# Clustered attention followed by a gated FFN on one core: contiguous loads, a half-batch pipeline, mask rows without DMA, weights staged in fp32

## The chip, the core and the metric

The kernel runs on one NeuronCore of a Trainium2 chip. The metric is device time in microseconds (us), the median of several runs. Before the change it is 446.86 us (three runs, 446.13 to 447.54).

Engine names: PE multiplies matrices (PEld is its weight load), DVE is the vector engine, ACT the scalar engine, POOL the GpSimd engine. SP only issues DMAs; "SPq" and "POOLq" are the instruction queues from which DMAs are issued.

## The reference

```python
B, H, S, D = 4, 8, 768, 64          # 16 clusters per head
q_assign = argmax(q_n @ c_n.T)      # cluster of each query (normalised vectors)
k_assign = argmax(k_n @ c_n.T)
scores   = where(q_assign[:, None] == k_assign[None, :], q @ k.T / 8, -1e9)
attn     = softmax(scores)
x        = (attn @ v) as (3072, 512)
out      = (silu(x @ w_gate) * (x @ w_val)) @ w_out     # d_ff 1536
```

All inputs are fp32. The three weight matrices are 9.4 MB together, q, k and v 18.9 MB.

## The kernel before

Work on PE comes in these pieces. A *head* is prepared by six transposes (q and k to feature-major). A *quad* of four heads is then routed: a matmul with the centroids, then a chain on DVE (transpose, maximum, compare, transpose back) that gives one-hot rows. These 16 rows are put under the 64 feature rows of q and of k, so that a single matmul of 80 rows gives the masked scores. A *unit* of attention is two score matmuls, one exp on ACT and two value matmuls. A head has three units for each half of the queries. A *half batch* is 24 units (8 heads), and it gives the 384 tokens of one FFN *chunk*. A chunk has 12 gate/value blocks (`gv`, 8 matmuls each) and 3 output blocks (`o_ps`, 12 matmuls each).

```python
def load_quad(qi):                       # q and k share one tile, interleaved
    for i in range(4):
        t = sb.tile([128, J, 2, 64], FP32, tag="qk", bufs=6)
        nc.sync.dma_start(out=t[:, :, 0, :], in_=q[b, h].rearrange("(p j) d -> p j d", p=128))
        nc.sync.dma_start(out=t[:, :, 1, :], in_=k[b, h].rearrange("(p j) d -> p j d", p=128))
# ... v and the weights: nc.gpsimd.dma_start(bf16 tile <- fp32 dram), converted on the way
load_quad(0); load_v(0); load_quad(1)
# ... centroids; load_v(1); all weights
def prep_route(qi):
    # ... matmul with centroids, DVE: transpose, max, compare
    nc.vector.transpose(out=ohT, in_=oh)
    for i in range(4):                   # mask rows go to their partitions by DMA
        nc.sync.dma_start(out=qaug[(b, h)][D:KA], in_=ohT[32 * i:32 * i + NCL, :])
        nc.sync.dma_start(out=kaug[(b, h)][D:KA], in_=ohT[32 * i + NCL:32 * i + 2 * NCL, :])
# ... att_scores, att_values; per pair of heads:
                nc.vector.reciprocal(out=den, in_=den)          # 128 x 384
                nc.gpsimd.tensor_tensor(out=xall[...], in0=num, in1=den, op=ALU.mult)
# ... main program
for f in prep_work(0): f[0](*f[1:])      # both quads of batch 0
for b in range(B):
    ffn = list(ffn_work(b - 1)) if b > 0 else []     # FFN one whole batch behind
    for ui, u in enumerate(units):                   # 48 units
        pt = att_scores(u)
        want = len(ffn) * (ui + 1) // n              # paced by number of blocks
        # ... emit FFN blocks up to want; att_values of the unit before
        want = len(prep) * max(0, ui + 1 - 12) // (n - 12)   # preparation spread evenly
        # ...
for f in ffn_work(B - 1): f[0](*f[1:])   # two chunks alone at the end
```

The softmax here doesn't subtract the row's maximum and nothing guards it: scores larger than these inputs give would overflow.

## Time and profile before

| Stretch (span 444.2 us) | What runs | What limits it |
|---|---|---|
| 0 to 50.8 us | loads, preparation of the first two quads | loads |
| 50.8 to about 105 us | attention of batch 0, no FFN | ACT, 49.8 of 54.2 us busy |
| 105 to 397 us | attention beside the FFN of the batch before | PE, with bubbles |
| 397 to 444 us | FFN of the last batch | PE |

The page of the kernel before, second part: forty equal slices of 11.1 us. Each digit is the busy share in tenths; PEclk is the clock granted to PE. The line of packets stands below the slices.

```profile
...
PE   3601778889889998999889998998889988989996
...
ACT  3200499898678577765677777756776677633231
...
PEclk9955599999999999999999999999999999999999
DMA  9999893579001434652003122110000100010101
GB/s 158 193 208 198 164 148 73 84 87 133 18 1 36 125 63 64 91 82 58 19 1 73 71 19 29 8 48 29 14 0 26 47 1 1 25 47 2 71 1 71
DMA packets 83838, 28.77 MB, mean 65 GB/s; under 512 B 77152, under 2 KB 79712, under 8 KB 83808
...
```

PE does little in the first four slices while the DMA line is full, and the granted clock is half in the third to the fifth. Of 83,838 packets, 77,152 carry less than 512 B.

The table of windows of the kernel before: start and end, length, then busy us and number of instructions (PE, PEld, DVE, ACT, POOL), granted clock, DMA share, GB/s.

```profile
...
0.00:50.80 50.80, 16.38 (x78) 10.54 (x78) 9.34 (x13) 9.65 (x12) 30.74 (x52) 0.72 1.17 192
50.80:105.00 54.20, 46.66 (x273) 24.79 (x271) 34.59 (x34) 49.84 (x71) 28.45 (x34) 0.98 0.70 108
...
```

The timeline of the kernel before, from its first 64 us: start, duration, engine, line, operation, and in brackets the idle time before it with what ended it.

```profile
...
16.23 9.06 SPq L94 DMA_DIRECT2D qk<-in_k_dram  x1
...
20.16 0.98 DVE L192 STREAM_TRANSPOSE ohT<-oh 128x768 bf16<-128x768 bf16 x1
...
26.51 11.98 SPq L94 DMA_DIRECT2D qk<-in_k_dram  x1
...
29.82 0.84 POOL L158 CAST qa<-qkT 64x768 bf16<-64x768 f32 x1
...
38.59 3.96 SPq L196 DMA_DIRECT2D qa<-ohT  x1
...
47.95 1.51 PE L150 MATMUL tp<-ident_f,qk 128*128 128x128 f32 x6 [2.60 <-DMA qk<-in_k_dram]
...
50.83 0.82 PE L212 MATMUL sc<-qa,ka 80*128 80x384 bf16 x2
...
```

The one-hot rows of the first quad are ready at 21.1 us. The first copy that carries them leaves at 38.6 us, because two q, k loads ahead of it occupy the SP queue for 9.1 and 12.0 us. The first scores come at 50.8 us.

The reciprocal in the list of groups, and four lines of the chain that ended last, kernel before. A group line gives line, engine, operation, out<-in with shapes, count, busy us, mean ns.

```profile
...
L254 DVE RECIPROCAL den<-den 128x384 f32<-128x384 f32 x32 | 81.6, 2550 | 0.5
...
```

```profile
...
143.35 2.65 PE o_ps L294 x12
...
240.31 2.65 PE o_ps L294 x12
...
340.58 2.59 PE o_ps L294 x12
...
385.17 2.59 PE o_ps L294 x12
...
```

In the chain lines (start, duration, what), the same output block of one batch and the next lies 97.0 us apart (143.35 to 240.31), and in the last batch, which prepares nothing, the last two half batches lie 44.6 us apart (340.58 to 385.17).

**The ledger.** PE's least work is worked out from dense stretches of the timeline: 0.65 us a unit, 1.30 us a gate/value block, 2.6 us an output block, 0.85 us a head's transposes, 1.47 us a quad's routing. 192 units, 96 and 24 blocks, 32 heads and 8 quads make 351 us. A stretch's length less the least work done in it is PE time lost. A batch with preparation needs 88 us, a half batch without it 39 us. So the kernel before loses 4.5 us in each half batch with preparation and 5.6 us without.

### The profile page before, as it was taken

To read this page: it belongs to the slowest core of one execution; us is meant where nothing else is said; L and a number is where in the kernel's file an instruction comes from. 1 tells how busy PE (TensorE), PEld (TensorE's weight loads), DVE (VectorE), ACT (ScalarE), POOL (GpSimd) and SP (SyncE) were. 2 spreads that over 40 slices of the span, in tenths; PEclk is the share of its full clock that TensorE was granted. 3 is DMA by queue.
4 is the path that set the end of the run, shared out by engine and by line. 5 is a ranking of instruction groups with operands and counts; after the bars stand their busy time and mean duration, and the time that the engine had idled before them with its cause. 6 is when DMAs were issued, how large, how long until landed. Compare 5 with 4: busy or idle time off the path is not lost.

```text
span 444.2 us, 6000 instructions
## 1 busy us (share of the span) xinstructions
PE 374.1 (84%) x2152; PEld 206.8 (47%) x2152; DVE 257.3 (58%) x343; ACT 274.6 (62%) x412; POOL 123.2 (28%) x157
## 2 busy tenths in 40 slices
PE   3601778889889998999889998998889988989996
PEld 2301345454445555544455555544454545445552
DVE  4400166676877188655875287728675567558280
ACT  3200499898678577765677777756776677633231
POOL 9455504575002333531103133320000000000000
PEclk9955599999999999999999999999999999999999
DMA  9999893579001434652003122110000100010101
GB/s 158 193 208 198 164 148 73 84 87 133 18 1 36 125 63 64 91 82 58 19 1 73 71 19 29 8 48 29 14 0 26 47 1 1 25 47 2 71 1 71
DMA packets 83838, 28.77 MB, mean 65 GB/s; under 512 B 77152, under 2 KB 79712, under 8 KB 83808
## 3 DMA queue, kind: packets, MB, share of 16 engines
q1 hardware_dynamic: 55968, 20.52, 19.0%
q0 software_dynamic: 27840, 7.87, 16.8%
q8 instruction: 17, 0.28, 0.3%
q14 instruction: 13, 0.11, 0.1%
HBM read 28.38 MB, written 6.29 MB: 78 GB/s over the span
## 4 chain that ended last, share of the span: by engine, by line
PE 53%; ACT 17%; DVE 14%; SPq 6%; DMA 5%; issue 3%; POOL 1%; ACTq 0%; DVEq 0%; POOLq 0%
PE o_ps L294 12%; PE gv L269 12%; PE gv L274 11%; PE sc L212 7%; DVE den L254 7%; PE acc L234 6%; DMA qk<-in_k_dram 5%; ACT den L247 5%; SPq L94 3%; PE sp L169 3%; ACT pt_83 L218 3%; ACT pt_85 L218 3%; ACT pt_84 L218 2%; ACT th L279 2%; SPq L92 2%
## 5 line engine op out<-in xcount | busy, mean ns | idle before, releaser
L212 PE MATMUL sc<-qa,ka 80*128 80x384 bf16 x384 | 93.4, 326 | 7.1 <-ACT qkT L155 2.8
L269 PE MATMUL gv<-xall,wg_sb 128*128 128x384 bf16 x384 | 78.0, 325 | 17.9 <-ACT pt_83 L218 5.7
L279 ACT ACTIVATE th<-gv 128x384 f32<-128x384 f32 x96 | 47.1, 491 | 58.5 <-PE gv L274 55.2
L254 DVE RECIPROCAL den<-den 128x384 f32<-128x384 f32 x32 | 81.6, 2550 | 0.5
L282 DVE SCALAR_TENSOR_TENSOR ug<-th,gv 128x384 f32<-128x384 f32 x96 | 52.0, 547 | 50.5 <-ACT th L279 49.3
L255 POOL TENSOR_TENSOR xall<-num,den 128x384 bf16<-128x384 f32 x32 | 31.9, 997 | 175.1 <-DVE den L254 174.5
L274 PE MATMUL gv<-xall,wv_sb 128*128 128x384 bf16 x384 | 78.1, 326 | 0.0
L250 DVE TENSOR_SCALAR num<-acc 64x384 f32<-64x384 f32 x64 | 39.9, 623 | 60.8 <-ACT den L247 59.8
L294 PE MATMUL o_ps<-wo_sb,hT 128*128 128x512 bf16 x288 | 66.2, 379 | 1.0 <-DVE hT L285 0.9
L150 PE MATMUL tp<-ident_f,qk 128*128 128x128 f32 x192 | 31.9, 306 | 34.4 <-DMA qk<-in_k_dram 34.4
L269 PEld LDWEIGHTS <-wg_sb 128*128 128x128 bf16 x384 | 37.0, 96 | 49.9 <-issue 27.1
L212 PEld LDWEIGHTS <-ka 80*128 80x128 bf16 x384 | 36.9, 98 | 38.2 <-issue 16.2
L285 DVE TENSOR_TENSOR hT<-ug,gv 128x384 bf16<-128x384 f32 x96 | 52.3, 550 | 2.4
L155 ACT ACTIVATE qkT<-tp 128x768 f32<-128x768 f32 x32 | 25.9, 810 | 42.6 <-PE tp L150 42.1
L274 PEld LDWEIGHTS <-wv_sb 128*128 128x128 bf16 x384 | 37.5, 98 | 24.9
L218 ACT ACTIVATE pt_83<-sc 128x768 bf16<-128x768 f32 x48 | 39.0, 812 | 9.1 <-PE sc L212 8.4
L150 PEld LDWEIGHTS tp<-ident_f,qk 128*128 128x128 f32 x192 | 26.1, 158 | 39.3 <-issue 35.6
L294 PEld LDWEIGHTS <-hT 128*128 128x128 bf16 x288 | 28.0, 97 | 35.2 <-DVE hT L285 3.2
L218 ACT ACTIVATE pt_85<-sc 128x768 bf16<-128x768 f32 x48 | 38.9, 811 | 7.3 <-PE sc L212 6.9
L218 ACT ACTIVATE pt_84<-sc 128x768 bf16<-128x768 f32 x48 | 39.0, 812 | 4.1 <-PE sc L212 3.2
L218 ACT ACTIVATE pt_86<-sc 128x768 bf16<-128x768 f32 x48 | 38.9, 811 | 2.2 <-PE sc L212 0.9
L175 DVE STREAM_TRANSPOSE sT<-sp 128x768 f32<-128x768 f32 x8 | 7.9, 983 | 54.1 <-PE sp L169 54.1
(62 smaller groups left out, 334.4 us busy)
## 6 DMA issues: line engine op xcount, KB each, us to landing
qk<-in_q_dram SPq DMA_DIRECT2D x32, 192.0 KB, 3.5
qk<-in_k_dram SPq DMA_DIRECT2D x32, 192.0 KB, 3.7
out_dram<-o_sb SPq DMA_DIRECT2D x24, 256.0 KB, 2.0
wg_sb<-in_moe_w_gate_dram POOLq DMA_DIRECT2D x4, 384.0 KB, 13.9
wv_sb<-in_moe_w_val_dram POOLq DMA_DIRECT2D x4, 384.0 KB, 14.7
wo_sb<-in_moe_w_out_dram POOLq DMA_DIRECT2D x4, 384.0 KB, 17.3
vaug_74<-in_v_dram POOLq DMA_DIRECT2D x12, 96.0 KB, 3.3
vaug_75<-in_v_dram POOLq DMA_DIRECT2D x12, 96.0 KB, 3.7
```

The lines of the kernel that those rows point to most:

```text
L150: nc.tensor.transpose(out=tp[:, j // JH, ts(j % JH, 128)], in_=t[:, j, :, :], identity=ident_f)
L212: nc.tensor.matmul(out=sc[:, jj, 0:SH], lhsT=ka[:, j // JH, ts(j % JH, 128)], rhs=qa[:, hf, :], start=True, stop=True)
L218: nc.scalar.activation(out=pt[:, :, 0:SH], in_=sc[:, :, 0:SH], func=ACT.Exp, scale=SCALE)
L250: nc.vector.tensor_scalar_add(num[n0:n0 + 64], acc[n0:n0 + 64, 0:SH], acc[n0:n0 + 64, SH:SH + 1])
L254: nc.vector.reciprocal(out=den, in_=den)
L255: nc.gpsimd.tensor_tensor(out=xall[:, h // 2, ds(b * S + hf * SH, SH)], in0=num, in1=den, op=ALU.mult)
L269: nc.tensor.matmul(out=gv[:, 0, 0:SH], lhsT=wg_sb[:, c, ts(fb, 128)], rhs=xall[:, c, ds(cb, SH)], start=(c == 0), stop=(c == DMC - 1))
L274: nc.tensor.matmul(out=gv[:, 1, 0:SH], lhsT=wv_sb[:, c, ts(fb, 128)], rhs=xall[:, c, ds(cb, SH)], start=(c == 0), stop=(c == DMC - 1))
L279: nc.scalar.activation(out=th, in_=gv[:, 0, 0:SH], func=ACT.Tanh, scale=0.5)
L282: nc.vector.scalar_tensor_tensor(out=ug, in0=th, scalar=1.0, in1=gv[:, 0, 0:SH], op0=ALU.add, op1=ALU.mult)
L285: nc.vector.tensor_tensor(out=hTs[ch][:, fb, :], in0=ug, in1=gv[:, 1, 0:SH], op=ALU.mult)
L294: nc.tensor.matmul(out=o_ps, lhsT=hT[:, fc, ts(ob, 128)], rhs=wo_sb[:, fc, :], start=(fc == 0), stop=(fc == DFC - 1))
```

## The change

The intent: get attention started earlier by faster loads, by taking the mask rows off the DMA queues and by starting after one quad; run the FFN half a batch behind instead of a whole one; pace the FFN by PE time; and keep long DVE instructions from holding up others. The diff, cut to its core:

```diff
 def load_quad(qi):
-    t = sb.tile([128, J, 2, 64], FP32, tag="qk", bufs=6)     # q and k interleaved, 256 B runs
-    nc.sync.dma_start(out=t[:, :, 0, :], in_=q...); nc.sync.dma_start(out=t[:, :, 1, :], in_=k...)
+    for src in (q, k):                                       # 1536 B runs on both sides
+        t = sb.tile([128, J, 64], FP32, tag="qk", bufs=12)
+        nc.sync.dma_start(out=t, in_=src[b, h].rearrange("(p j) d -> p j d", p=128))
 # v: fp32 tile through SP, cast on Pool.  Weights: 18 jobs of 512 KB through two fp32 buffers
-nc.gpsimd.dma_start(out=wg_sb[:, c, :], in_=wgr[:, c, :])   # ... 12 converting DMAs
+wt = sb.tile(..., FP32, tag="wt", bufs=2); nc.sync.dma_start(out=wt, in_=src)
+eng = nc.vector if i % 2 == 0 else nc.gpsimd
+eng.tensor_copy(out=wjobs[i][1], in_=wst.pop(i))
 # transposes: q alone and k alone, even tokens on partitions 0-63, odd on 64-127
 # mask rows: a second DVE transpose, shifted by 16 columns, puts the odd tokens' rows on the same partitions
+for par in range(2):
+    nc.vector.transpose(out=ohT[:, par], in_=oh[:, par:par + 48, :])
-nc.sync.dma_start(out=qaug[(b, h)][D:KA], in_=ohT[32 * i:32 * i + NCL, :])   # and k
+nc.gpsimd.tensor_copy(out=qkaug[(b, h)][D:KA, par], in_=ohTs[qi][32 * i:32 * i + NCL, par])
-nc.vector.reciprocal(out=den, in_=den)
+for r in range(3): nc.vector.reciprocal(out=den[:, ts(r, 128)], in_=den[:, ts(r, 128)])
 # main program: one list of 192 units; FFN 24 + LAG units behind, LAG = 4
+for f in prep(0): f[0](*f[1:])                               # one quad only
+want = per * (ui - NU - LAG + 1) / NU                        # output block counts 2, gate/value block 1
+for n, f in enumerate(prep(NQ * b)):     put(u0 + (18 + 2 * n if n < 5 else 24 + n), *f)
+for n, f in enumerate(prep(NQ * b + 1)): put(u0 + (36 + 2 * n if n < 5 else 42 + n), *f)
```

## The prediction

> **What bounds the kernel now:** three stages (windows table, chain of waits, timeline).
>
> 1. 0 to 50.8 us, start: PE busy 16.4 us, clock 0.72. The first scores run at 50.8 us. The timeline shows the first quad's one-hot rows ready at 21.1 us, but the small copies that carry them to their partitions stand in the SP queue behind q, k loads, stuck for 9.1 and 12.0 us while weights arrive; they go from 38.6 us on. DMA is full: 77,152 of 83,838 packets are below 512 B.
> 2. 50.8 to 105 us, first batch's attention without FFN: ACT busy 49.8 of 54.2 us.
> 3. 105 to 397 us: PE-bound with bubbles. 397 to 444 us: FFN alone, dense.
>
> PE's least work, from dense stretches of the timeline: a unit of scores and values 0.65 us (192: 125 us), a gate/value block 1.30 and an output block 2.6 us (96 and 24: 187 us), a head's transposes 0.85, a quad's routing 1.47 us (39 us): 351 us. A batch with preparation needs 88 us and takes 97, the last 78 and 95: 4.5 to 8 us lost per half batch, much of it behind the 2.55 us reciprocal (6.8% of the chain).
>
> **What the change does.**
> - Loads in runs of 1 to 2 KB. The Trainium skill, "DMA: Bandwidth & Descriptors", section "Why small descriptors are slow (HBM only)", gives a fixed cost per packet, 27% at 256 B. The trace agrees in kind: start-up loads move about 200 GB/s with the engines full; output stores of 2 KB rows move 71 GB/s at a 0.19 share, an estimate of 370 full.
> - Mask rows leave DMA: one more 0.95 us DVE transpose per quad, two Pool copies per head (taken as 0.82 us, like the casts: 52 us). v casts (0.45) and half the weight casts (1.1) go to Pool; 34 us of DMA issue leaves. Pool: 123 to about 165 us, limiting only in the first half batch.
> - Attention starts after one quad: loads 5 to 9 us, transposes to 11.5, routing to 15, DVE to 20, two Pool copies to 22.
> - Only half a batch (24 units, about 26 us) is ACT-bound without FFN; FFN then lags by 4 units. The tail is one chunk (23.4 us).
> - Weights: two staging buffers, a pair takes about 5 us (landing 3.5, cast 1, issue), so gate and value weights are in near 60 us, wo near 75; FFN wants them from 54 us on, progressively. Little wait.
> - The reciprocal in three pieces costs nearly nothing and lets FFN vector work pass.
>
> **Sum.** 22 + 26 + 2 (crowded Pool) = 50 us. PE then has 351 - 16 (first half) - 10 (two quads) = 325 us. Bubbles of seven half batches at 4 to 5 us: 31. Lag and tail 4. Outside the span 2. Total 412 us; the range 400 to 428 us should hold it 8 in 10. Faster by over 2%: 0.93; within 2%: 0.06; slower: 0.01.
>
> **What would show it.** First scores near 22 us; no one-hot DMAs; packets below 512 B nearly gone; first gate matmul near 54 us (before: 108); ACT above 85% only until then; dense tail of about 28 us; reciprocals near 0.85 us with a smaller share of the chain; PE's least work unchanged.
>
> **What would make it wrong.** Weight casts on DVE blocking the release of accumulators when loads land late (first half batch 40 us); Pool's 1.64 us per head of mask copies delaying quad 1; FFN's first block waiting for the last head's normalisation each half batch; more bubbles because seven chunks now run beside attention: then 428 to 440 us. If bubbles fall to 2 us per half batch, 396 us.

## More of the kernel before

The framework orders the instructions of each engine before the run, by its own forecast of when their inputs are ready. At run time each engine keeps that order.

## The result, and the profile after

| | before | after |
|---|---|---|
| time, median of 3 | 446.86 us | 410.10 us (408.41 to 410.17) |
| ratio | | 0.9166 (0.9123 to 0.9208) |
| span of the profiled run | 444.2 us | 408.0 us |
| first scores | 50.8 us | 23.8 us |
| first gate/value block | 108.3 us | 67.5 us |
| batch with preparation | 97.0 us | 91.7 us |
| half batch without preparation | 44.6 us | 41.9 us |

A ratio is the mean time of one kernel's fast runs over that of the kernel before in the same rounds, so it is not quite the ratio of the medians. In the experiments below, a difference in us to the changed kernel is the difference of the two ratios times 446.9. Differences of about 2 us are not clear of the noise.

The ledger of the two kernels, and of a last version that is told at the end of the experiments (work per stretch from the counts of matmuls that the table of windows gives for each line, units by their score matmuls; 14 output matmuls that the changed kernel's trace lacks are counted in; each figure is good to about half a us):

| PE time lost, us | before | predicted | after | last version |
|---|---|---|---|---|
| until the first scores | 42.0 | 17 | 18.9 | 11.4 |
| first scores to first gate/value block | 14.6 | 9 | 14.4 | 13.6 |
| from there to the end | 36.8 | 33 | 23.8 | 21.7 |
| sum (351 more is the span) | 93.4 | 59 | 57.1 | 46.7 |

The column "predicted" comes from the prediction's own times in the same way: 22 us less a quad (4.9 us); the 32 us up to 54 us less 28 units and a quad (18.2 and 4.9, together 23.1 us); 356 us from there to the end of a span of 410 less the remaining 323.

The page of the changed kernel, second part and the line of packets:

```profile
...
PE   5268787799999999999999999999999999999996
...
ACT  5048596677677675877677675877677677767331
...
PEclk9869599999999999999999999999999999999999
DMA  8986888434120032234120030000010001000102
GB/s 260 309 268 190 275 251 265 161 109 124 47 71 2 0 116 93 63 109 124 47 72 2 0 104 31 23 0 2 26 53 1 0 27 51 2 0 27 52 0 79
DMA packets 25566, 35.06 MB, mean 86 GB/s; under 512 B 2496, under 2 KB 20928, under 8 KB 25536
...
```

The idle start is shorter, the packets below 512 B have gone from 77,152 to 2,496, and the start moves up to 309 GB/s where it moved 208. PE is at nine tenths from the ninth slice on. One slice, 40.8 to 51 us, has the clock at half.

The timeline of the changed kernel, first 36 us:

```profile
...
15.17 1.19 DVE L215 TENSOR_TENSOR oh_156<-sT,rmax 128x384 bf16<-128x384 f32 x1
16.28 1.17 DVE L219 SCALAR_TENSOR_TENSOR oh_156<-sT,rs 128x384 bf16<-128x384 f32 x1
...
19.19 1.86 DVE L165 CAST wg_sb<-wt 128x1024 bf16<-128x1024 f32 x1 [1.74 <-DMA wt<-in_moe_w_gate_dram]
...
20.97 1.82 DVE L225 STREAM_TRANSPOSE ohT<-oh_156 128x768 bf16<-128x768 bf16 x2
...
22.91 7.00 POOL L233 COPY qka<-ohT 16x768 bf16<-16x768 bf16 x8
...
23.78 0.82 PE L246 MATMUL sc<-qka 80*128 80x384 bf16 x2 [10.75 <-POOL qka L233]
...
```

The one-hot values are done at 17.45 us (16.28 and 1.17), but DVE's next instruction is a weight cast that waits until 19.19 us for its load. The transposes behind it end at 22.8 us. Then Pool copies the rows and the first scores start. The Trainium skill says that DVE's queue is strictly first in, first out ("TensorE: Matmul & The Clock Gate", section "Architectural detail: the array is 16× 32×32, not 1× 128×128"); the trace agrees: the ready transpose waits 3.5 us behind the cast.

Who waited for whom on DVE, 18 to 75 us, changed kernel (engine, line, waited for, us in total, times, longest):

```profile
...
DVE wg_sb L165 <- DMA wt<-in_moe_w_gate_dram: 10.7, 5, 4.5
...
```

DVE stands 10.7 us in front of weight loads, once for 4.5 us.

The timeline of the changed kernel around unit 12, PE only, and two windows, one inside PE's wait and one after it (columns as above):

```profile
...
39.22 0.49 PE L269 MATMUL acc<-pt_133,vaug_93 128*128 128x385 bf16 x2
43.23 0.82 PE L246 MATMUL sc<-qka 80*128 80x384 bf16 x2 [3.52 <-POOL qka L233]
...
```

```profile
...
41.00:42.00 1.00, 0.00 (x0) 0.00 (x0) 1.00 (x2) 0.30 (x1) 0.99 (x3) 0.80 0.64 141
...
43.00:52.00 9.00, 8.77 (x28) 3.99 (x29) 5.45 (x8) 5.71 (x8) 8.54 (x11) 0.51 0.82 284
...
```

PE waits 3.5 us for the second quad's mask rows, and the granted clock is 0.51 in the nine us after that. The Trainium skill describes this gate ("TensorE: Matmul & The Clock Gate", section "Part 1: The HAM clock gate (the "warmup" mystery)"): about 3.4 us without work and the clock halves, about 3.4 us of work and it is full again. Neither length is seen here. The clock is full from 40 to 41 us and 0.80 on average from 41 to 42: it falls at about 41.6 us, 1.9 us into the wait. It is full again at about 51.8 us, 8.6 us after PE took up work; after the first scores, 4.2 us were enough (23.8 to 27.9 us). In the run masks_by_dma below it fell at 46.0 us although no wait of PE in the four us before was longer than 0.8 us; PE was busy for 1.64 of the last 3.41 us.

The group line of the reciprocals, and how they lie in the timeline of the changed kernel:

```profile
...
L290 DVE RECIPROCAL den<-den 128x128 f32<-128x128 f32 x96 | 82.4, 913 | 0.4
...
```

```profile
...
223.47 2.58 DVE L290 RECIPROCAL den<-den 128x128 f32<-128x128 f32 x3
226.08 1.02 DVE L319 SCALAR_TENSOR_TENSOR ug<-th,gv 128x384 f32<-128x384 f32 x2
```

The three pieces run back to back: 2.58 us where one took 2.55. Nothing passes between them in the steady state.

The chain of the changed kernel, output blocks one batch apart, and of two half batches without preparation:

```profile
...
147.92 2.16 PE o_ps L331 x10
...
239.66 2.16 PE o_ps L331 x10
...
329.57 2.38 PE o_ps L331 x11
...
371.51 2.38 PE o_ps L331 x11
...
```

### The profile page after: what moved, and what is told of

Read it like the earlier page. It is cut to its first block, busy times and chain, and to the rows that moved or that the text cites. A ratio compares the mean times of both kernels' runs of the same rounds, so it can differ in the third digit from the quotient of the medians.

```text
span 408.0 us, 6039 instructions
## 1 busy us (share of the span) xinstructions
PE 368.2 (90%) x2131; PEld 207.2 (51%) x2145; DVE 271.5 (67%) x432; ACT 273.6 (67%) x412; POOL 169.6 (42%) x213
## 2 busy tenths in 40 slices
DMA packets 25566, 35.06 MB, mean 86 GB/s; under 512 B 2496, under 2 KB 20928, under 8 KB 25536
## 4 chain that ended last, share of the span: by engine, by line
PE 69%; ACT 8%; POOL 7%; DMA 7%; DVE 6%; issue 2%; POOLq 0%; SPq 0%; ACTq 0%
PE gv L306 15%; PE o_ps L331 14%; PE gv L311 14%; PE sc L246 12%; PE acc L269 11%; ACT pt_132 L253 4%; DMA wt<-in_moe_w_out_dram 4%; POOL qka L186 4%; DVE den L290 3%; PE tp L179 2%; PE sp L201 2%; ACT den L282 1%; DVE num L285 1%; DMA vs<-in_v_dram 1%; ACT th L316 1%
## 5 line engine op out<-in xcount | busy, mean ns | idle before, releaser
L246 PE MATMUL sc<-qka 80*128 80x384 bf16 x384 | 95.4, 333 | 15.6 <-POOL qka L233 14.3
L290 DVE RECIPROCAL den<-den 128x128 f32<-128x128 f32 x96 | 82.4, 913 | 0.4
L186 POOL CAST qka<-qkT 64x768 bf16<-64x768 f32 x64 | 55.0, 859 | 43.0 <-ACT qkT L183 41.0
L331 PE MATMUL o_ps<-wo_sb,hT 128*128 128x512 bf16 x274 | 64.6, 379 | 1.6 <-DVE num L285 1.0
L246 PEld LDWEIGHTS <-qka 80*128 80x128 bf16 x384 | 37.6, 100 | 45.5 <-POOL qka L233 16.0
L233 POOL COPY qka<-ohT 16x768 bf16<-16x768 bf16 x64 | 52.9, 840 | 14.3 <-DVE ohT L225 12.2
L253 ACT ACTIVATE pt_132<-sc 128x768 bf16<-128x768 f32 x48 | 39.0, 812 | 20.2 <-PE sc L246 19.1
L311 PEld LDWEIGHTS <-wv_sb 128*128 128x128 bf16 x384 | 37.5, 98 | 26.5 <-issue 1.7
L282 ACT ACTIVATE den<-acc,eps 64x384 f32<-64x384 f32 x64 | 36.9, 576 | 3.4 <-PE acc L269 1.8
L335 ACT ACTIVATE o_sb<-o_ps 128x512 f32<-128x512 f32 x24 | 14.3, 597 | 31.3 <-PE o_ps L331 31.3
```

Of the source, the lines that this page charges most:

```text
L186: nc.gpsimd.tensor_copy(out=qka[0:D, par, :, :], in_=qkT[64 * par:64 * par + 64])
L233: nc.gpsimd.tensor_copy(out=qkaug[(b, 4 * g + i)][D:KA, par], in_=ohTs[qi][32 * i:32 * i + NCL, par])
L246: nc.tensor.matmul(out=sc[:, jj, 0:SH], lhsT=qka[:, j // JH, 1, ts(j % JH, 128)], rhs=qka[:, hf, 0, :], start=True, stop=True)
L253: nc.scalar.activation(out=pt[:, :, 0:SH], in_=sc[:, :, 0:SH], func=ACT.Exp, scale=SCALE)
L290: nc.vector.reciprocal(out=den[:, ts(r, 128)], in_=den[:, ts(r, 128)])
L311: nc.tensor.matmul(out=gv[:, 1, 0:SH], lhsT=wv_sb[:, c, ts(fb, 128)], rhs=xall[:, cb, c, :], start=(c == 0), stop=(c == DMC - 1))
```

## The experiments

Twelve kernels ran, and all gave correct results.

| run | median us | ratio (95%) | to the changed kernel |
|---|---|---|---|
| one_reciprocal | 408.77 | 0.9141 (0.9122 to 0.9160) | -1.1 us |
| lag_a_whole_batch | 412.51 | 0.9216 (0.9197 to 0.9235) | +2.2 us |
| before_weighted_pacing | 448.13 | 1.0016 (0.9995 to 1.0037) | (kernel before) |
| first_masks_on_dve | 409.02 | 0.9174 (0.9134 to 0.9214) | +0.4 us |
| packets_of_256_bytes | 424.10 | 0.9490 (0.9458 to 0.9521) | +14.5 us |
| two_quads_first | 407.66 | 0.9134 (0.9102 to 0.9165) | -1.4 us |
| masks_by_dma | 413.38 | 0.9251 (0.9200 to 0.9303) | +3.8 us |
| weights_by_pool_dma | 414.05 | 0.9277 (0.9243 to 0.9310) | +5.0 us |
| pool_casts_weights | 408.76 | 0.9148 (0.9118 to 0.9178) | -0.8 us |
| routing_in_gate_phase | 413.40 | 0.9242 (0.9222 to 0.9262) | +3.4 us |
| before_aligned_routing | 436.24 | 0.9778 (0.9741 to 0.9816) | (kernel before) |
| free_dve_two_quads | 398.32 | 0.8920 (0.8907 to 0.8933) | -11.0 us |

### The steady state

The theory: bubbles shrink because the split reciprocal lets FFN work pass. Rivals: the pacing by PE time, the half-batch lag, or the place of the routing.

**one_reciprocal.**

```diff
-for r in range(JH): nc.vector.reciprocal(out=den[:, ts(r, 128)], in_=den[:, ts(r, 128)])
+nc.vector.reciprocal(out=den, in_=den)
```

> The changed kernel with one 384-wide reciprocal instead of three of 128. If the split is what lets FFN vector work pass and cut the bubbles (the prediction's step): 416 to 422 us, ratio to before 0.93 to 0.945, half batches of 48 to 49 us instead of 46. If the pieces run back to back, as the trace of the changed kernel shows (2.58 us for three against 2.55 for one): 409 to 411 us, ratio 0.914 to 0.920, half batches unchanged.

It took 408.77 us, and the batch distance is 91.7 us, unchanged. The split brings nothing; that step of the prediction falls.

**lag_a_whole_batch.**

```diff
-LAG = 4
+LAG = 28
```

> The changed kernel with the FFN 28 units behind attention instead of 4, so that a whole batch runs without FFN and two chunks stand alone at the end. If the half-batch pipeline is worth the ACT-bound half it removes: 418 to 425 us. If PE work is only moved (the second half without FFN needs 25 us of PE and 26 of ACT, and the extra chunk of the tail runs dense): 410 to 413 us.

412.51 us, as the second expectation had it. A whole second half batch without FFN costs only some 2 us, not clear of the noise, because what it loses is mostly regained in a longer dense tail. The half-batch pipeline, the most visible part of the change, is worth little.

**before_weighted_pacing**, in the kernel before.

```diff
-want = len(ffn) * (ui + 1) // n
-while df < want:
+wgt = [2 if f[0] is ffn_out else 1 for f in ffn]
+want = sum(wgt) * (ui + 1) // n
+while df < len(ffn) and sum(wgt[:df + 1]) <= want:
```

> The kernel before, with one edit: FFN blocks are paced by PE time (an output block counts 2, a gate/value block 1) instead of by number. If the smaller bubbles come from pacing: 428 to 438 us (2 to 3 us less in each of six half batches), ratio 0.96 to 0.98. If they come from the other parts (reciprocal, masks off the SP queue, shorter lag): 445 to 448 us, ratio 0.997 to 1.003.

448.13 us, no gain in total. But the parts differ: a half batch without preparation went from 44.6 to 43.0 us, a batch with it from 97.0 to 98.5. With pacing alone, PE waits for DVE's hT (1.4 us before `gv`, 5.2 us before the scores, between 110 and 380 us; the kernel before 0.3 and 1.6 us), which pointed at the routing chain on DVE.

**before_aligned_routing**, the kernel before with the same pacing and the preparation at chosen units.

```diff
-want = len(prep) * max(0, ui + 1 - 12) // (n - 12)
+at = (12, 14, 16, 17, 19, 36, 38, 40, 41, 43)      # the fifth and tenth are the routings
+want = sum(a <= ui for a in at) if prep else 0
```

> The kernel before with weighted pacing (which alone gave nothing) and the preparation placed so that routing falls among the output blocks. If this placement is what makes the bubbles small: a batch takes 92 to 94 us instead of 97, total 436 to 442 us, ratio 0.975 to 0.988. If not: 445 to 449 us.

436.24 us, a gain of 2.2% over the kernel before (interval 1.8 to 2.6%), with nothing else of the change in it. The chain, output blocks one batch apart and two half batches of the last batch:

```profile
...
140.54 2.54 PE o_ps L294 x11
...
233.79 2.54 PE o_ps L294 x11
...
325.37 2.16 PE o_ps L294 x10
...
368.35 2.16 PE o_ps L294 x10
...
```

A batch takes 93.2 us instead of 97.0, a half batch without preparation 43.0 instead of 44.6. Twice 3.8 and twice 1.6 make 10.8 us, which is the whole gain (10.6 us by the medians, 9.9 by the ratio).

**routing_in_gate_phase**, the opposite in the changed kernel: preparation of batches 2 and 3 is moved forward.

```diff
+o1, o2 = (12, 6) if b > 1 else (0, 0)
-put(u0 + (18 + 2 * n if n < 5 else 24 + n), *f)          # and 36, 42
+put(u0 - o1 + (18 + 2 * n if n < 5 else 24 + n), *f)     # and u0 - o2 + 36, 42
```

> The changed kernel with the preparation of batches 2 and 3 moved 12 and 6 units earlier, so that the routing (5.3 us of DVE) falls among the gate/value blocks instead of the output blocks; nothing else. If the small bubbles (1.9 us per half batch with preparation, 4.5 before) come from routing lying where DVE is otherwise idle: four half batches grow by 2 to 3 us, total 418 to 422 us. If placement does not matter: 409 to 411 us.

413.40 us: slower, in the expected direction, but by 3.4 us and not 8 to 12. The chain, output blocks one batch apart:

```profile
...
151.06 1.99 PE o_ps L331 x9
...
244.44 1.99 PE o_ps L331 x9
...
```

A batch takes 93.4 us instead of 91.7. Two batches were touched, and twice 1.7 us are the 3.4 us.

What follows: in the steady state the place of the routing and the pacing together do most of it. Before: DVE's gate/value work and the routing chain (4.1 us for the first quad) came at the same time, while DVE is idle during output blocks (7.2 us in one stretch of the kernel before). The waits of PE that the profile lists between 110 and 380 us fit this: in the kernel before, `gv` waits 15.9 us for ACT's exp, and 2.5 us are waits for DVE's hT; with the pacing alone it is 9.8 and 6.6 us, with the placement too 8.8 and 1.6 us. So the pacing takes away waits for ACT and adds waits for DVE, and the placement takes the latter away again. These waits are only part of the lost time, so the mechanism on DVE is in part a reading; that the two edits together give the gain is shown. The pacing without the placement gained nothing; the placement without the pacing was not run, so whether it needs the pacing is not shown. The remaining 1.5 us per batch between before_aligned_routing (93.2) and the changed kernel (91.7) was not isolated. It also stays open why the move in the changed kernel cost less than the two edits gained.

### The start

**packets_of_256_bytes.** Token j*128+p goes to partition p, so that runs in memory are 256 B, as the pieces of q and k were before; the tiles stay contiguous.

```diff
-src[b, h].rearrange("(p j) d -> p j d", p=128)      # q, k, v
+src[b, h].rearrange("(j p) d -> p j d", p=128)
-outr = out.rearrange("(b p j) d -> b j p d", b=B, j=J)
+outr = out.rearrange("(b j p) d -> b j p d", b=B, j=J)
```

> The changed kernel with q, k, v read token j*128+p into partition p, so that every run in memory is 256 B again; all else and the results are the same. If packet size is the main part of the start's gain: first scores at 35 us or later (23.8 now), total over 425 us. If order matters more (one quad first, masks and weights off the congested queues): first scores at 26 to 29 us, total 411 to 418 us.

424.10 us: neither expectation holds in full. The total is near the first one's, the mechanism is not: the first scores come *earlier* (19.1 us), since here the order of DVE's instructions puts no weight cast before the transposes. The loss comes after that. From the page, and the waits of PE from 24 to 84 us:

```profile
...
DMA packets 87006, 35.06 MB, mean 83 GB/s; under 512 B 76224, under 2 KB 82368, under 8 KB 86976
...
```

```profile
...
PE tp L179 <- DMA qk<-in_q_dram: 11.0, 3, 4.8
PE tp L179 <- DMA qk<-in_k_dram: 4.3, 2, 2.8
...
```

PE stands 15.3 us before transposes of the *next* batch, which lie in its order ahead of the first FFN block, and whose loads are late. The first gate/value block comes at 83.5 instead of 67.5 us. The steady state is the same (91.8 us a batch). Between 5 and 24 us the loads move 218 GB/s with the DMA engines full; the changed kernel moves 302 GB/s there on average, and up to 401. Of the parts undone singly, the packet size is thus the largest.

**two_quads_first.**

```diff
-for n, f in enumerate(prep(1)): put(n if n < 5 else n + 2, *f)
+for f in prep(1): f[0](*f[1:])
```

> The changed kernel with the second quad prepared before attention starts, as before. If starting after one quad is a large part of the gain: total 418 to 424 us. If the second quad's preparation mostly fills PE time that is idle at the start anyway: within 3 us of 410.

407.66 us, 1.4 us less than the changed kernel, within the noise. Starting after one quad gains nothing that shows: the first scores came at 24.2 us here too, because the second quad fills PE time in which it only waits for the first quad's chain on DVE and Pool.

**masks_by_dma.**

```diff
-nc.gpsimd.tensor_copy(out=qkaug[(b, 4 * g + i)][D:KA, par], in_=...)
+nc.sync.dma_start(out=qkaug[(b, 4 * g + i)][D:KA, par], in_=...)
```

> The changed kernel with the mask rows carried by small DMAs on the SP queue again instead of Pool copies. If taking masks off the SP queue is a large part of the gain: first scores at 30 us or later, long waits of scores for a DMA at the first heads and at unit 12, total 416 to 430 us. If not: 408 to 412 us, Pool 53 us less busy.

413.38 us, 3.8 us slower, between the two expectations; first scores at 26.5 us. Who PE waited for, 0 to 72 us:

```profile
...
PE sc L246 <- DMA qka<-ohT: 15.2, 2, 14.4
...
```

Mask rows on the SP queue cost little once the loads no longer clog it. In the kernel before they were late because of the loads.

**weights_by_pool_dma.**

```diff
+for c in range(DMC): nc.gpsimd.dma_start(out=wg_sb[:, c, :], in_=wgr[:, c, :])   # wv, wo alike
-# staging through wt and all casts
```

> The changed kernel with the weights brought by twelve converting DMAs of the Pool queue at the start, as before, and no staging or casts. If these DMAs are what filled the start and held up the SP queue: first scores at 35 us or later, total 422 to 440 us. If the 256 B loads were what congested it: first scores at 22 to 25 us, and since DVE no longer stands in order behind weight loads, first gate matmul at 55 to 60 us instead of 67.5, total 400 to 406 us.

414.05 us, 5.0 us slower, so again between. First scores at 28.1 us; the first gate/value block at 71.9 us. The timeline of POOL, and PE's longest wait up to 30 us:

```profile
...
20.12 7.00 POOL L193 CAST qka<-qkT 64x768 bf16<-64x768 f32 x8
...
```

```profile
...
PE sc L253 <- POOL qka L240: 12.6, 1, 12.6
...
```

POOL issues the weight DMAs and waits 8.7 us in front of the last four of them, so its casts of the first quad's q and k begin at 20.1 us; in the changed kernel they begin at 10.7 us, in the kernel before at 29.8 us. PE's wait here is for POOL's order, not for the SP queue.

**first_masks_on_dve.**

```diff
-nc.gpsimd.tensor_copy(
+eng = nc.vector if qi < 2 else nc.gpsimd
+eng.tensor_copy(
```

> The changed kernel with the mask rows of the first two quads copied by DVE instead of Pool (16 copies[...]). If Pool paces the first half batch: the wait at unit 12 (3.5 us) goes, the clock does not fall there, the first gate matmul comes at 57 to 60 us instead of 67.5, total 400 to 404 us. If the weights' two staging buffers (a pair every 4.5 to 5 us, the chain from 53.7 to 75 us) pace it: first gate matmul at 64 us or later, total 407 to 410 us.

409.02 us, no gain, first gate/value block at 66.9 us. The copies had a median of 352 ns on DVE, and PE still waited 2.9 us before unit 12, now for DVE. Pool's mask copies alone do not pace the first half batch. Here the chain runs through DVE and the weight loads: 20.1% of it up to 75 us are loads of w_out and 19.1% of w_gate.

**pool_casts_weights.** All weight casts on Pool; q, k casts and mask copies of quads 0 and 1 on DVE.

```diff
-eng = nc.vector if i % 2 == 0 else nc.gpsimd
-eng.tensor_copy(out=wjobs[i][1], in_=wst.pop(i))
+nc.gpsimd.tensor_copy(out=wjobs[i][1], in_=wst.pop(i))
+eng = nc.vector if qi < 2 else nc.gpsimd      # for the q, k casts and the mask copies
```

> The changed kernel with all 18 weight casts on Pool, and in exchange the first two quads' q, k casts and mask copies on DVE: no instruction in DVE's order waits for a weight load any more. If DVE standing behind weight loads is what stretched the first half batch (28 us forecast, 43.7 measured): first scores at 20 to 22 us, first gate matmul at 54 to 60 us, total 398 to 404 us. If the arrival of the weights or the load of the DMA engines paces it: first gate matmul at 64 us or later, total 407 to 411 us.

408.76 us. The first scores came at 20.2 us as expected and DVE waits for no weight load any more, but the first gate/value block moved only to 63.0 us and the total hardly at all. Freeing DVE is not enough by itself. The second expectation gave the total, the first gave the start.

**free_dve_two_quads.** The edits of two_quads_first, first_masks_on_dve and one_reciprocal, all weight casts on Pool, and the q, k casts of quad 0 only on DVE.

> Five edits of the changed kernel together: two quads prepared first, all weight casts on Pool, the first quad's q, k casts and the first two quads' mask copies on DVE, one reciprocal. If what is still lost before the FFN starts (about 14 us of PE time between 23.8 and 67.5 us) comes from DVE standing behind weight loads and from Pool's crowd: first scores near 21 us, first gate matmul at 54 to 60 us, total 402 to 405 us, below the changed kernel by over 1%. If the PE work that is left then (first chunk beside the next batch's preparation) or the loads set the pace: total 406 to 409 us, as two quads alone.

398.32 us, 11.0 us under the changed kernel, better than either expectation, and faster than both kernels. First scores at 21.1 us, first gate/value block at 59.1 us. In the ledger, 7.5 us of this come before the first scores, where the second quad is now prepared in the wait, and only 0.8 us in the stretch after it; 2.1 us come later. The parts alone gave -1.4, +0.4, -1.1 and, in a form with more casts on DVE, -0.8 us. So they do not add up: the same start is freed only when they are taken together. The granted clock goes with it: 0.991 on average over the profiled run, 0.974 in the changed kernel. Which pair of them suffices was not tried.

A group of this run shows what the mask copies cost on DVE beside Pool (min, median and max of one instruction in ns):

```profile
...
L234 POOL COPY qka<-ohT x48: 817/822/827, 63.8 to 287.4; 16x768 bf16<-16x768 bf16 x48
L234 DVE COPY qka<-ohT x16: 342/742/1182, 20.2 to 36.8; 16x768 bf16<-16x768 bf16 x16
...
```

```profile
...
20.24 7.14 DVE L234 COPY qka<-ohT 16x768 bf16<-16x768 bf16 x8
...
33.47 3.64 DVE L234 COPY qka<-ohT 16x768 bf16<-16x768 bf16 x8
...
```

Eight copies take 7.14 us while Pool runs its casts, and 3.64 us later when Pool is mostly waiting; alone one takes 342 ns. The Trainium skill has the reason ("GPSIMD Engine Reference", section "8. Key points"): Pool shares its SBUF interfaces with DVE and contends with two-input and two-port instructions. The trace agrees, and also in the changed kernel, where the first quad's two compares took 1.19 and 1.17 us beside Pool's casts, and all compares from 70 us on, with nothing on Pool beside them, 0.54 to 0.55 us.

## Why the prediction was right or wrong

The time was 410.1 us for a forecast of 412, and the total lost was 57.1 us for 59. Two terms were off, in opposite directions.

- **Right: the start.** First scores at 23.8 us for 22; lost 18.9 for 17. The chain of loads, transposes, routing, DVE and Pool is as described. The weight cast in front of the transposes (3.5 us) more than covers the difference.
- **Right for another reason: why the start was late before.** The prediction put the mask copies in the SP queue first, and gave the small packets no share of their own. The copies were late, but masks_by_dma costs only 3.8 us. The 256 B packets cost 14.5 us and the converting weight DMAs, which keep POOL from its casts, 5.0 us, each undone alone. And PE stood in its order before the second quad's loads. "Attention starts after one quad" gains nothing (two_quads_first).
- **Wrong: "24 units, about 26 us", and "first gate matmul near 54 us".** It came at 67.5 us, and the stretch before it lost 14.4 us instead of 9. The trace shows DVE 10.7 us behind weight loads, PE 3.5 us before the mask rows of unit 12, and the clock at 0.51 for nine us. The hazards were on the list ("Weight casts on DVE", "Pool's 1.64 us per head of mask copies delaying quad 1"), but they were not put into the sum. ACT was at nine tenths in one slice only (the sixth), not throughout: the table of windows has it busy 21.1 of 30.0 us between 24 and 54 us. Part of the delay is no loss: about two more units and four heads of the next batch had run by then.
- **Wrong: "bubbles of seven half batches at 4 to 5 us".** They are 1.9 us with preparation (91.7 less 88, over two) and 2.9 without. So the stretch from the first block to the end lost 23.8 us, not 33.
- **Wrong: the step "the reciprocal in three pieces ... lets FFN vector work pass".** The pieces run back to back and one_reciprocal is no slower. What shrank the bubbles is pacing with the routing among output blocks, as before_aligned_routing shows: about 10 us in the kernel before.
- **Right in kind: the tail and the half batch.** One chunk is left at the end. It is worth only about 2 us (lag_a_whole_batch), which agrees with the small loss that the prediction's sum gave to an ACT-bound half batch, not with the weight that its text gave it.

The right total therefore rests partly on two errors that cancel: about 5 us too little lost in the first half batch, about 9 too much later.

Singly undone, packets, weight DMAs, mask copies and lag make 14.5 + 5.0 + 3.8 + 2.2 = 25.5 us; pacing and placement gave about 10 us in the kernel before. The sum is near the 37 us of the change. This is a check of size, not a proof, since the last version shows that parts need not add up, and since the new paths of v and of the centroids were undone in no run.

## What to carry to other kernels

An in-order engine should never hold, ahead of work that others wait for, an instruction that waits for a bulk load; and when a start is limited in several such places, single repairs can show almost nothing until they are made together, as here. Make the ledger of least work per stretch before crediting a change: the half-batch pipeline and the split reciprocal looked like the core of this one and were worth about 2 us and nothing. Put the long vector chain of a side task into the stretch where PE's main work needs no vector engine.

## What the Trainium skill lacked or had wrong

- "DMA: Bandwidth & Descriptors", section "Why small descriptors are slow (HBM only)": it gives 27% overhead per packet at 256 B. Here loads in 256 B runs moved 218 GB/s with the engines full; the changed kernel's longer runs moved 358 to 360 GB/s between 5 and 15 us, with the engines full too, and 401 at most. The loss was thus 39 to 46%, more than the 27% (the section names a second cost, of descriptor data, without a share).
- "GPSIMD Engine Reference", section "8. Key points": this section names the contention with DVE but no size (the rule for it stands on another page of the skill). Measured: a DVE copy of 16x768 bf16 from 342 to 1182 ns, a two-input compare of 128x384 from 542 to 1185 ns. The 0.84 us that the slowest copy lost is about one instruction of Pool (0.82 to 1.16 us).
- "VectorE: DVE Perf Modes", section "The perf-mode tier table (the rule you actually need)": its fast rate for a bf16 copy within SBUF fits the 342 ns copy (an estimate from its 693 ns for 2048 elements, with the 150 cycles of fixed cost that the page gives elsewhere: about 356 ns), but the page says nothing of a busy Pool, beside which eight copies in free_dve_two_quads took 655 to 1182 ns. With Pool mostly idle, in first_masks_on_dve, the median was 352 ns.
- "TensorE: Matmul & The Clock Gate", section "Part 1: The HAM clock gate (the "warmup" mystery)": an idle window of about 3.4 us should halve the clock, and 3.4 us of activity should restore it. In the changed kernel it fell 1.9 us into a wait and stayed at half for 8.6 us of work (43.2 to 51.8 us). In masks_by_dma it fell with PE busy for 1.64 of the last 3.41 us.
